# Fill the fourth tile of query rows up to whole groups, load queries one tile ahead, and issue the second scatters behind the first splits

## The chip, the cores and the metric

One core of one Trainium2 chip runs the program. The metric is the device time of one execution in microseconds. Engines work beside each other and wait for one another through semaphores: TensorE (PE, with its weight loads as PEld), VectorE (DVE), ScalarE (ACT), GpSimd (POOL) and SyncE (SP). DMA transfers are issued from the queues of SP and ACT; an issue takes the queue some time, and an issue that waits holds up all that stand behind it in that queue.

## What is computed

Attention whose heads are mixed by a 12 x 12 matrix before the softmax and by another one after it, followed by two feed-forward layers on its output (4 x 448 tokens, 768 wide).

```
scores = scale * np.matmul(q, k.transpose(0, 1, 3, 2))     # 4 batches, 12 heads, 448 x 448, head size 64
scores = np.einsum('bhij,hg->bgij', scores, w_pre)
scores = scores - np.max(scores, axis=-1, keepdims=True)
attn = np.exp(scores)
attn = attn / (np.sum(attn, axis=-1, keepdims=True) + 1e-09)
attn = np.einsum('bhij,hg->bgij', attn, w_post)
x = np.matmul(attn, v)
...
x = (1.0 / (1.0 + np.exp(-(x @ w_gate))) * (x @ w_val)) @ w_out
h = np.maximum(x @ w_in, 0.0)
out = (h * h) @ w_out2
```

## The kernel before

The mixing over heads is a matrix product whose contraction runs over (row, head) pairs: ten query rows (GI = 10) times twelve heads fill 120 partitions, with a block-diagonal matrix as weight. Such ten rows are a *group*. A batch of 448 rows is cut into four *tiles* of 110, 110, 110 and 118 rows (`row_tiles`); the first three are eleven groups each, the fourth eleven groups and one of eight rows. Two tiles are a *chunk*, for which the value products run together.

`scores(n, p)` makes the scores of tile n for the pair of heads p: two products into PSUM, a copy of each to an SBUF buffer `e` (one on ScalarE, one on VectorE), and a *scatter* of each, a DMA from `e` (a row of the tile on each partition) into `g` (a partition for each row-in-group and head, the groups one behind the other). So that a scatter is one regular access, the host lays the query rows out in the order of `row_order`: first the row 0 of all groups, then row 1, and so on. Where the tile has rows beyond whole groups, they follow at the end, and a second small DMA (line 196, the *tail*) scatters them. The very first tile is laid out as two blocks (groups 0 to 3 and 4 to 10), whose second scatters are collected in the list `second` and issued later (line 357), so that the first groups can start early.

`split(s)` then takes group s of `g` apart into a high and a low half (`gh` on ScalarE, `gl` on GpSimd), `premix(s)` makes three products of them, `maximum`, `exponent` and `normal` the softmax, `postmix(s)` the mixing after it, and `values(c, h)` the value products of chunk c for a pair of heads, with `vraw` from `v_load`: two heads a buffer, four buffers, so of the six loads of a chunk the fifth and sixth wait for the first and second pair of value products. `valued` copies the result out (`xo`) and stores it to DRAM (`xs`).

The order of everything is written out by hand, in a loop over s, the groups of all batches. Each step issues the premix of group s, the split of group s + 2, and, as its budget of TensorE time allows, postmixes, value products and the scores of the next tile; `next_scores` issues the scores of a pair of heads and, in the fourth tile of a batch, behind them a load of `k` for the next batch. In that loop the queries of tile n + 1 are loaded (`q_load`, two buffers) behind the last pair of heads of tile n. Nearly all DMAs go through SyncE's queue in the order of the program; only some scatters of the very first tile are issued by ScalarE. The feed-forward part (`mlp`) is fed into the last steps of that loop and then runs alone.

Of the kernel before, what the change touches and what calls it, by code (L numbers as in the profile page):

```python
# [18 lines left out]
GI = 10  # L19
# [17 lines left out]

def blocks(b, i0, i1):

    n = (i1 - i0) // GI  # L40
    return [(0, 4), (4, n)] if b == i0 == 0 else [(0, n)]


def row_order(b, i0, i1):

    rows = []
    for g0, g1 in blocks(b, i0, i1):
        rows += [i0 + g * GI + r for r in range(GI) for g in range(g0, g1)]
    return rows + list(range(i0 + len(rows), i1))


def attention(tc, q, k, v, w_pre, w_post, xs, B, H, S, D):
# [10 lines left out]
    nc = tc.nc  # L63
    JT = S // JP
    NP = H // 2
    SCALE = 1.0 / float(D) ** 0.5

    tiles, groups, chunks = [], [], []
# [7 lines left out]
            chunks[-1][4] = len(groups)  # L76
            tiles.append((b, i0, i1 - i0))
    NG = len(groups)
    IM = max(t[2] for t in tiles)
    GT = -(-IM // GI)  # L80
    CM = max(c[2] - c[1] for c in chunks)
    KM = GI * H

    with ExitStack() as ctx, ExitStack() as mid, ExitStack() as left:
# [55 lines left out]
        k_t, q_t = {}, {}  # L140
# [3 lines left out]
            nc.sync.dma_start(out=k_t[b, p], in_=k[b, p])  # L144

        def q_load(n, p0=0, p1=NP):
            b, i0, isz = tiles[n]
            if p0 == 0:
                q_t[n] = p2.tile([P, NP, IM], F32, tag="q", name="q")
            n0, n1 = (b * S + i0) * H * D, (b * S + i0 + isz) * H * D  # L150
            x = q[n0:n1].rearrange("(d p i) -> d p i", d=P, p=NP)
            nc.sync.dma_start(out=q_t[n][:, p0:p1, :isz], in_=x[:, p0:p1])


        g_t, second = {}, []

        def scores(n, p):

            b, i0, isz = tiles[n]
            if p == 0:  # L160
                g_t[n] = pg.tile([KM, GT, S], F32, tag="g", name="g")
            kt = k_t.pop((b, p)) if i0 + isz == S else k_t[b, p]
            ps = [
                ps_b.tile([P, S], F32, tag="b", name="ps_s")
                if n == 0 and p % 2
                else ps_q.tile([P, S], F32, tag="q", name="ps_s")
                for _ in range(2)
            ]
            for o in range(2):
                r = slice(o * D, (o + 1) * D)  # L170
                nc.tensor.matmul(  # L171
                    ps[o][:isz], lhsT=q_t[n][r, p, :isz], rhs=kt[r], start=True, stop=True
                )
            if n == 0 and p >= 3:
                e = [pa.tile([IM, S], F32, tag="a", name="e0") for _ in range(2)]
            else:
                t = p4.tile([IM, 2, S], F32, tag="e", name="e")
                e = [t[:, o] for o in range(2)]
            to = g_t[n].rearrange("(r h) g j -> h r g j", h=H)
            for o in range(2):  # L180
                if o:
                    nc.vector.tensor_copy(e[o][:isz], ps[o][:isz])
                else:
                    nc.scalar.copy(e[o][:isz], ps[o][:isz])
                e0 = 0
                for m, (g0, g1) in enumerate(blocks(b, i0, i0 + isz)):
                    e1 = e0 + (g1 - g0) * GI
                    move = (to[2 * p + o, :, g0:g1], e[o][e0:e1])
                    if m:
                        second.append(move)  # L190
                    else:
                        queue = nc.scalar if n == 0 and o and p in (1, 3, 4, 5) else nc.sync
                        queue.dma_start(out=move[0], in_=move[1])
                    e0 = e1
                if e0 < isz:
                    nc.sync.dma_start(out=to[2 * p + o, : isz - e0, g1], in_=e[o][e0:isz])


        a_t = {}
# [109 lines left out]
        NT = len(tiles)  # L309
# [24 lines left out]
        def next_scores():  # L334
            _, _, n, h = front.pop(0)
            scores(n, h)
            if tiles[n][1] + tiles[n][2] == S:
                load_next(k_load, k_order)
            if h == NP - 1 and n + 1 < NT:
                q_load(n + 1)  # L340

        def flush():
# [4 lines left out]
        for p in range(0, NP, 2):  # L347
            q_load(0, p, p + 2)
            load_next(k_load, k_order)
            load_next(k_load, k_order)  # L350
        q_load(1)
        masks()
        for p in range(NP):
            scores(0, p)
        mixers()
        for m, (x, y) in enumerate(second):
            (nc.scalar if m % 3 == 1 else nc.sync).dma_start(out=x, in_=y)  # L357
        for s in range(2):
            split(s)
        for s in range(NG + 30):  # L360
            if s < NG:
                premix(s)
            flush()
            if s < NG:
                maximum(s)
            if s in (4, 5, 6, 7):
                load_next(v_load, v_order)
            if 8 <= s < 8 + KB - NP:
                load_next(k_load, k_order)
            if 1 <= s <= NG:  # L370
                exponent(s - 1)
            if 2 <= s < NG + 2:
                normal(s - 2)
            if s + 2 < NG:
                split(s + 2)
            left_over = STEP - MW
            ready = front and front[0][0] <= s
            if ready and due(s):
                next_scores()
                ready, left_over = False, left_over - SW  # L380
            while bpos < len(back) and (left_over > 0.5 or s >= NG):
                f, cost, *x = back[bpos]
                if f is postmix:
                    if x[0] > s - LAG:
                        break
                    posted[groups[x[0]][3]] = s
                elif posted[x[0]] == s:
                    if s < NG:
                        break
                    flush()  # L390
                elif posted[x[0]] == s - 1 and ready:
                    next_scores()
                    ready = False
                if len(pending) > 3:
                    flush()
                f(*x)
                if f is values and (x[1] + 2) % HV == 0:
                    pending.append((load_next, v_load, v_order))
                bpos += 1
                left_over -= cost  # L400
                if f is postmix and x[0] == NG - 1:
                    flush()
                    mid.close()
                if s >= NG:
                    yield 3 if bpos == len(back) or back[bpos][0] is values else 2
            if ready and left_over > 0.4:
                next_scores()
            if not front and not closed:
                left.close()
                closed = True  # L410
            if NG - EARLY <= s < NG:
                behind += 1
                if closed:
                    yield 2
                elif behind >= 3 and s not in posted.values():
                    behind -= 3
                    yield 1
# [406 lines left out]
```

## Time and profile before

| | |
|---|---|
| median of three runs | 1508.63 us (1508.27 to 1511.84) |
| profiled execution | 1510.66 us, of it 1508.9 us span |
| PE busy | 1468.7 us, 97% of the span |
| PE on the chain that ended last | 95% |
| DVE, ACT, POOL busy | 809.2, 579.6, 708.8 us |
| DMA | 185.47 MB in 87976 packets, 123 GB/s in the mean |

TensorE is busy in nearly the whole span, so the profile is read for the places where it waits. The page gives shares of the whole; the stage in question, attention, takes about the first 540 us, and there the timelines, the waits and the stretches tell more. In a timeline a row is an instruction, or several alike merged (x16), with its start and length; a bracket at its end says how long its engine was idle before it and what released it. Where a wait had several reasons, the bracket names one of them, which need not be the one that came last.

### The profile page before, as it was taken

To read this page: it belongs to the slowest core of one execution; us is meant where nothing else is said; L and a number is where in the kernel's file an instruction comes from. 1 tells how busy PE (TensorE), PEld (TensorE's weight loads), DVE (VectorE), ACT (ScalarE), POOL (GpSimd) and SP (SyncE) were. 2 spreads that over 40 slices of the span, in tenths; PEclk is the share of its full clock that TensorE was granted. 3 is DMA by queue.
4 is the path that set the end of the run, shared out by engine and by line. 5 is a ranking of instruction groups with operands and counts; after the bars stand their busy time and mean duration, and the time that the engine had idled before them with its cause. 6 is when DMAs were issued, how large, how long until landed. Compare 5 with 4: busy or idle time off the path is not lost.

```text
span 1508.9 us, 22075 instructions
## 1 busy us (share of the span) xinstructions
PE 1468.7 (97%) x8028; PEld 1245.0 (83%) x8028; DVE 809.2 (54%) x1367; ACT 579.6 (38%) x1192; POOL 708.8 (47%) x583
## 2 busy tenths in 40 slices
PE   6989989999998999999999999999999999999999
PEld 3657657667676889999999999999999999999998
DVE  4648657667678577778889999911111001333000
ACT  4545645655655333333234433312222122333111
POOL 3646656766679355555455555532222221222221
PEclk8989999999999999999999999999999999999999
DMA  5453553545534354444444446631211111112221
GB/s 178 140 163 113 150 156 119 168 132 172 167 116 141 113 170 174 156 166 164 158 157 159 163 166 205 217 96 53 63 43 62 53 53 53 53 53 67 75 72 39
DMA packets 87976, 185.47 MB, mean 123 GB/s; under 512 B 18236, under 2 KB 55100, under 8 KB 87868
## 3 DMA queue, kind: packets, MB, share of 16 engines
q1 hardware_dynamic: 87348, 183.28, 38.4%
q8 instruction: 63, 1.03, 0.3%
q10 hardware_dynamic: 520, 0.79, 0.2%
q14 instruction: 45, 0.37, 0.1%
HBM read 107.75 MB, written 37.75 MB: 96 GB/s over the span
## 4 chain that ended last, share of the span: by engine, by line
PE 95%; DMA 2%; POOL 1%; DVE 1%; issue 1%; SPq 0%; ACT 0%; ACTq 0%; POOLq 0%; DVEq 0%
PE ps L666 66%; PE ps_p L261 9%; PE ps_m L219 8%; PE ps_s L171 6%; PE ps_v L290 5%; DMA vraw<-in_v 1%; DMA q<-in_q 0%; POOL gl L210 0%; POOL wn L246 0%; DMA g<-e 0%; DVE ap L273 0%; DMA k<-in_k 0%; ACTq L357 0%; POOL wl L534 0%; DVE nm L227 0%
## 5 line engine op out<-in xcount | busy, mean ns | idle before, releaser
L534 POOL TENSOR_TENSOR wl<-w,wh 128x768 fp32r<-128x768 f32 (+1 forms) x140 | 257.6, 1842 | 550.8 <-ACT wh L526 542.4
L666 PE MATMUL ps<-xh,wh 128*128 128x448 f32 x960 | 351.1, 366 | 0.0
L666 PE MATMUL ps<-xh,wl 128*128 128x448 f32 x960 | 350.7, 365 | 0.0
L666 PE MATMUL ps<-xl,wh 128*128 128x448 f32 x960 | 350.6, 365 | 0.0
L666 PE MATMUL ps<-hh,wl 128*128 128x448 f32 x672 | 246.8, 367 | 0.0
L666 PE MATMUL ps<-hl,wh 128*128 128x448 f32 x672 | 246.8, 367 | 0.0
L666 PE MATMUL ps<-hh,wh 128*128 128x448 f32 x672 | 246.7, 367 | 0.0
L210 POOL TENSOR_TENSOR gl<-g,gh 120x448 fp32r<-120x448 f32 x180 | 208.6, 1160 | 22.2 <-DMA g<-e 18.6
L261 PEld LDWEIGHTS ps_p<-wn,a 120*112 120x112 f32 (+1 forms) x1440 | 165.0, 178 | 43.2 <-issue 20.7
L666 PEld LDWEIGHTS ps<-xh,wh 128*128 128x128 f32 x960 | 180.3, 188 | 15.5 <-issue 1.0
L666 PEld LDWEIGHTS ps<-xh,wl 128*128 128x128 f32 x960 | 180.3, 188 | 14.4 <-POOL wl L534 0.2
L666 PEld LDWEIGHTS ps<-xl,wh 128*128 128x128 f32 x960 | 180.3, 188 | 14.2
L261 PE MATMUL ps_p<-wn,a 120*112 120x120 f32 (+1 forms) x1440 | 177.0, 271 | 6.9 <-POOL wn L246 6.8
L246 POOL TENSOR_SCALAR wn<-wq,sm 120x120 f32<-120x120 f32 x180 | 107.2, 596 | 148.9 <-DVE sm L244 115.4
L520 POOL TENSOR_TENSOR w<-w,w_f 128x768 f32<-128x768 f32 (+1 forms) x70 | 135.4, 1934 | 59.0 <-DVE w_f L509 59.0
L227 DVE TENSOR_REDUCE nm<-ps_m 120x1 f32<-120x448 f32 x180 | 112.0, 622 | 78.9 <-PE ps_m L219 78.6
L684 DVE TENSOR_TENSOR ps<-ps,sg 128x448 f32<-128x448 f32 x48 | 30.4, 632 | 197.2 <-PE ps L666 197.2
L666 PEld LDWEIGHTS ps<-hl,wh 128*128 128x128 f32 x672 | 126.1, 188 | 11.6
L666 PEld LDWEIGHTS ps<-hh,wh 128*128 128x128 f32 x672 | 126.1, 188 | 11.6
L666 PEld LDWEIGHTS ps<-hh,wl 128*128 128x128 f32 x672 | 126.1, 188 | 11.6
L235 ACT ACTIVATE a<-ps_m,nm 120x448 f32<-120x448 f32 x180 | 115.0, 639 | 48.0 <-DVE nm L227 46.6
L273 DVE COPY ap<-ps_p 112x480 f32<-112x480 f32 x180 | 117.0, 653 | 27.2 <-PE ps_p L261 27.2
(45 smaller groups left out, 1693.7 us busy)
## 6 DMA issues: line engine op xcount, KB each, us to landing
g<-e SPq DMA_DIRECT2D x180, 192.5 KB
ws<-w SPq DMA_DIRECT2D x58, 384.0 KB
w<-ws SPq DMA_DIRECT2D x58, 384.0 KB
w_raw<-in_wo SPq DMA_DIRECT2D x18, 768.0 KB
w_raw<-in_wi SPq DMA_DIRECT2D x16, 768.0 KB
vraw<-in_v SPq DMA_DIRECT2D x48, 224.0 KB
w_raw<-in_wg SPq DMA_DIRECT2D x12, 768.0 KB
w_raw<-in_wv SPq DMA_DIRECT2D x12, 768.0 KB
```

The source lines that it names most:

```text
L171: nc.tensor.matmul(ps[o][:isz], lhsT=q_t[n][r, p, :isz], rhs=kt[r], start=True, stop=True)
L210: nc.gpsimd.tensor_tensor(out=lo[:kk], in0=x, in1=hi[:kk].bitcast(F32), op=ALU.subtract)
L219: nc.tensor.matmul(ps[:kk], lhsT=wp[w][:kk, :kk], rhs=x, start=m == 0, stop=m == 2)
L227: nc.vector.tensor_reduce(out=nm[:kk], in_=ps[:kk], op=ALU.max, axis=AX.X, negate=True)
L235: nc.scalar.activation(a[:kk], ps[:kk], AF.Exp, bias=nm[:kk], accum_out=sm[:kk])
L246: nc.gpsimd.tensor_scalar(out=wn[:kk], in0=wq[:kk], scalar1=sm[:kk], scalar2=None, op0=ALU.mult)
L261: nc.tensor.matmul(ps[:JP, jt], lhsT=a[:kk, jt * JP : (jt + 1) * JP], rhs=wn[:kk].rearrange("p g i -> p (g i)"), start=True, stop=True,)
L273: nc.vector.tensor_copy(ap[c][:, :, :, g0 - i0 : g0 - i0 + rows], ps[:JP, :, :, :rows])
L290: nc.tensor.matmul(ps[o * D : (o + 1) * D, :w], lhsT=vraw[c, (h + o) // HV][:, (h + o) % HV, jt, :], rhs=ap[c][:, jt, h + o, :w], start=jt ...
L520: nc.gpsimd.tensor_tensor(out=x[:, s], in0=x[:, s], in1=fs.pop(n)[:, s], op=ALU.add)
L534: nc.gpsimd.tensor_tensor(out=lo[:, s], in0=w32.pop(n)[:, s], in1=h[:, s].bitcast(F32), op=ALU.subtract)
L666: nc.tensor.matmul(ps, lhsT=a, rhs=x, start=first and n == 0, stop=last and n == total - 1)
```

## The change

The fourth tile becomes twelve whole groups. `row_order` repeats the last row of the tile where a group runs over its end, so the host lays out 120 rows for 118; the queries are loaded, multiplied, copied and scattered with these two extra rows, and one scatter a head carries all of it. The tail DMA is gone. The mixing of the twelfth group goes on using its eight real rows.

In the loop, the queries of tile n + 1 are loaded behind the first pair of heads of tile n instead of the last. The queries of the second tile of all are loaded behind the first tile's scatters instead of ahead of them.

At the start, the second scatters of the first tile are issued behind the first two splits instead of ahead of them, and ScalarE issues two of them (the fourth and the eighth) instead of four.

```diff
 def blocks(b, i0, i1):
 
-    n = (i1 - i0) // GI
+    n = -(-(i1 - i0) // GI)
     return [(0, 4), (4, n)] if b == i0 == 0 else [(0, n)]
...
     for g0, g1 in blocks(b, i0, i1):
-        rows += [i0 + g * GI + r for r in range(GI) for g in range(g0, g1)]
-    return rows + list(range(i0 + len(rows), i1))
+        rows += [min(i0 + g * GI + r, i1 - 1) for r in range(GI) for g in range(g0, g1)]
+    return rows
...
-    IM = max(t[2] for t in tiles)
-    GT = -(-IM // GI)
+    full = [-(-t[2] // GI) * GI for t in tiles]
+    IM = max(full)
+    GT = IM // GI
...
         def q_load(n, p0=0, p1=NP):
-            b, i0, isz = tiles[n]
...
-            n0, n1 = (b * S + i0) * H * D, (b * S + i0 + isz) * H * D
+            n0, isz = sum(full[:n]) * H * D, full[n]
+            n1 = n0 + isz * H * D
...
         def scores(n, p):
 
-            b, i0, isz = tiles[n]
+            b, i0, rows = tiles[n]
+            isz = full[n]
...
-                for m, (g0, g1) in enumerate(blocks(b, i0, i0 + isz)):
+                for m, (g0, g1) in enumerate(blocks(b, i0, i0 + rows)):
...
-                if e0 < isz:
-                    nc.sync.dma_start(out=to[2 * p + o, : isz - e0, g1], in_=e[o][e0:isz])
...
-            if h == NP - 1 and n + 1 < NT:
+            if h == 0 and n + 1 < NT:
                 q_load(n + 1)
...
-        q_load(1)
         masks()
         for p in range(NP):
             scores(0, p)
+        q_load(1)
         mixers()
-        for m, (x, y) in enumerate(second):
-            (nc.scalar if m % 3 == 1 else nc.sync).dma_start(out=x, in_=y)
         for s in range(2):
             split(s)
+        for m, (x, y) in enumerate(second):
+            (nc.scalar if m in (3, 7) else nc.sync).dma_start(out=x, in_=y)
```

The first place is the end of the fourth tile of the first batch in SyncE's queue, from its fifth pair of heads on. A row is an issue, destination and source with their numbers, and the destination's shape; L193 is a scatter, L196 a tail, L144 a load of `k`, L152 of `q`, L306 the store of a value result, L280 a load of `vraw`. Before:

```order
L193 DMA g_821<-e_1001 10x11x448
L196 DMA g_821<-e_1001 8x448
L193 DMA g_821<-e_1001 10x11x448
L196 DMA g_821<-e_1001 8x448
L144 DMA k_1008<-in_k 128x448
L152 DMA q_1010<-in_q 128x6x110
L306 DMA xs0_57<-xo_1025 128x220
L280 DMA vraw_1028<-in_v 112x512
L306 DMA xs0_57<-xo_1056 128x220
L280 DMA vraw_1059<-in_v 112x512
```

In the same queue now (the line numbers are those of the changed kernel):

```order
L198 DMA g_821<-e_964 10x12x448 x2
L148 DMA k_969<-in_k 128x448
L198 DMA g_821<-e_993 10x12x448 x2
L148 DMA k_998<-in_k 128x448
L309 DMA xs0_57<-xo_1013 128x220
L283 DMA vraw_1016<-in_v 112x512
L309 DMA xs0_57<-xo_1044 128x220
L283 DMA vraw_1047<-in_v 112x512
```

Ahead of the fifth `vraw` load two tails a pair of heads are gone, and the load of `q`, which has moved up to the tile's first pair.

The second place is SyncE's queue at the start, from the last first-block scatter of the first tile to the scatters of the second. Before (the second tile's `q` was issued earlier, ahead of `wr`, as the row `q_146`):

```order
L193 DMA g_153<-e0_205 10x4x448
L357 DMA g_153<-e_158 10x7x448
L357 DMA g_153<-e_167 10x7x448 x2
L357 DMA g_153<-e_176 10x7x448
L357 DMA g_153<-e0_185 10x7x448
L357 DMA g_153<-e0_195 10x7x448
L357 DMA g_153<-e0_196 10x7x448
L357 DMA g_153<-e0_206 10x7x448
L193 DMA g_247<-e_252 10x11x448 x2
L193 DMA g_247<-e_274 10x11x448 x2
```

Now:

```order
L198 DMA g_151<-e0_203 10x4x448
L156 DMA q_209<-in_q 128x6x110
L362 DMA g_151<-e_156 10x7x448 x2
L362 DMA g_151<-e_165 10x7x448
L362 DMA g_151<-e_174 10x7x448 x2
L362 DMA g_151<-e0_183 10x7x448
L362 DMA g_151<-e0_193 10x7x448
L362 DMA g_151<-e0_194 10x7x448
L362 DMA g_151<-e0_203 10x7x448
L362 DMA g_151<-e0_204 10x7x448
L198 DMA g_247<-e_252 10x11x448 x2
L156 DMA q_257<-in_q 128x6x110
```

The second tile's `q` (`q_209`) now stands behind the first block, ten second scatters in place of eight follow it, and the third tile's `q` (`q_257`) stands behind the second tile's first two scatters.

The third place is ScalarE at the start, where its second-block scatters stood ahead of the first casts `gh`. Before:

```order
L193 DMA g_153<-e0_206 10x4x448
L357 DMA g_153<-e_158 10x7x448
L357 DMA g_153<-e_176 10x7x448
L357 DMA g_153<-e0_186 10x7x448
L357 DMA g_153<-e0_205 10x7x448
L209 CAST gh_229<-g_153 120x448
L209 CAST gh_233<-g_153 120x448
```

Now:

```order
L198 DMA g_151<-e0_204 10x4x448
L212 CAST gh_217<-g_151 120x448
L212 CAST gh_221<-g_151 120x448
L362 DMA g_151<-e_165 10x7x448
L362 DMA g_151<-e0_184 10x7x448
```

Two casts come first, and two second scatters follow in place of four.

## Rows read from the trace of the kernel before

**Rows 1.** Waits of PE: engine, line, waited for: us in total, times, longest

```profile
PE ps_v L290 <- DMA vraw<-in_v: 13.9, 4, 7.0
PE ps_m L219 <- ACT gh L209: 8.0, 1, 8.0
PE ps_s L171 <- DMA q<-in_q: 2.5, 1, 2.5
```

**Rows 2.** Timeline of PE, fourth tile, first batch: start us, us, engine, line, operation

```profile
83.12 1.02 PE L171 MATMUL ps_s<-k,q 64*118 64x448 f32 x4
...
88.95 1.71 PE L290 MATMUL ps_v<-ap,vraw 112*64 112x220 f32 x16
...
91.39 1.71 PE L290 MATMUL ps_v<-ap,vraw 112*64 112x220 f32 x16
...
100.89 3.20 PE L290 MATMUL ps_v<-ap,vraw 112*64 112x220 f32 x16 [7.00 <-DMA vraw<-in_v]
...
108.59 1.80 PE L261 MATMUL ps_p<-wn,a 120*112 120x120 f32 x16
```

**Rows 3.** Timeline of SP's queue: the start, and the fourth tile's end

```profile
5.18 0.67 SPq L152 DMA_DIRECT2D q<-in_q  x1
...
16.75 6.68 SPq L357 DMA_DIRECT2D g<-e  x8
...
89.15 0.77 SPq L193 DMA_DIRECT2D g<-e  x1
89.97 0.66 SPq L196 DMA_DIRECT2D g<-e  x1
90.73 0.39 SPq L144 DMA_DIRECT2D k<-in_k  x1
...
94.85 0.62 SPq L152 DMA_DIRECT2D q<-in_q  x1
...
96.24 0.38 SPq L280 DMA_DIRECT2D vraw<-in_v  x1
```

**Rows 4.** Timeline of PE, second and third batch, the same place

```profile
214.48 1.71 PE L290 MATMUL ps_v<-ap,vraw 112*64 112x220 f32 x16
...
228.57 1.80 PE L261 MATMUL ps_p<-wn,a 120*112 120x120 f32 x16
...
334.48 1.71 PE L290 MATMUL ps_v<-ap,vraw 112*64 112x220 f32 x16
...
345.68 1.80 PE L261 MATMUL ps_p<-wn,a 120*112 120x120 f32 x16
```

**Rows 5.** Timeline of PE, first scores of the third tile

```profile
45.27 1.46 PE L171 MATMUL ps_s<-k,q 64*110 64x448 f32 x4 [2.53 <-DMA q<-in_q]
...
49.42 1.01 PE L171 MATMUL ps_s<-k,q 64*110 64x448 f32 x4
...
51.97 1.01 PE L171 MATMUL ps_s<-k,q 64*110 64x448 f32 x4
```

**Rows 6.** Timeline of ACT: the start, the twelfth group's cast, a value copy

```profile
14.09 3.40 ACTq L357 DMA_DIRECT2D g<-e  x4
19.81 1.50 ACT L209 CAST gh<-g 120x448 fp32r<-120x448 f32 x3 [6.09 <-DMA g<-e]
...
44.01 0.56 ACT L209 CAST gh<-g 120x448 fp32r<-120x448 f32 x1 [2.58 <-POOL wn L246]
...
86.22 0.35 ACT L305 COPY xo<-ps_v 128x220 f32<-128x220 f32 x1
```

**Rows 7.** The chain that ended last, 0 to 50 us: start us, us, what

```profile
38.17 7.05 DMA q<-in_q
```

**Rows 8.** Stretches: us, busy by engine (instructions), granted PE clock, DMA share, GB/s

```profile
30.00:40.00 10.00, 9.77 (x64) 6.91 (x64) 8.22 (x20) 7.20 (x18) 7.42 (x10) 1.00 0.70 207
...
84.00:94.00 10.00, 9.89 (x78) 6.10 (x76) 3.65 (x14) 5.59 (x17) 6.59 (x8) 1.00 0.60 183
...
101.00:109.00 8.00, 8.00 (x43) 5.17 (x44) 1.06 (x4) 2.42 (x8) 1.68 (x2) 0.62 0.31 87
```

More of the change, by code (lines that the diff above doesn't have):

```diff
@@ L157, in scores @@
         def scores(n, p):
-            b, i0, isz = tiles[n]
+            b, i0, rows = tiles[n]
+            isz = full[n]
             if p == 0:
                 g_t[n] = pg.tile([KM, GT, S], F32, tag="g", name="g")
-            kt = k_t.pop((b, p)) if i0 + isz == S else k_t[b, p]
+            kt = k_t.pop((b, p)) if i0 + rows == S else k_t[b, p]
             ps = [
```

## The prediction

> **What bounds the kernel now.** TensorE is busy nearly everywhere, so I looked first for the places where it is not: the waits of TensorE [rows 1]. Three of its entries touch the change: four waits of the value products on `vraw` (13.9 us in all, the longest 7.0), one of the score products on `q` (2.5 us), and the first mix, held 8.0 us by the first cast `gh`, which itself waits for the first scatters. I then took each place in the timelines.
>
> *Fourth tile of a batch.* The value products of the chunk before run at the end of the fourth tile's scores, one pair of heads every 2.44 us (88.95 to 91.39, [rows 2]). Four pairs have their `vraw` in SBUF. The fifth load can be issued once the first pair is done; it should run at 91.39 + 2.44 = 93.83 and runs at 100.89. After the wait its 16 products take 3.20 us in place of 1.71: TensorE's granted clock, 0.62 in the mean from 101 to 109 [rows 8], is at its lower level, 1.2 GHz, for most of that stretch. The first double mix-back starts at 108.59; at three steps of 2.44 it would start at 98.71. This place costs **9.88 us**. Why is `vraw` late? SyncE's queue [rows 3] issues back to back: a scatter takes 0.82 us of it (89.15 to 89.97), its tail of eight rows 0.76 (89.97 to 90.73) for a fourteenth of the bytes. A pair of heads, four issues and a `k` load of some 0.45 (0.39 and the gap), takes 3.6 us of queue against the 2.56 us in which TensorE makes a pair of scores (49.42 to 51.97, [rows 5]), so the queue falls behind by about 1 us a pair, six times; then comes the `q` load (94.85), a store, and `vraw` at 96.24. The store's source was copied out at 86.22 to 86.57 [rows 6]. So `vraw` stood in line for over 9 us, and its landing (100.89 less 96.24, 4.65 with the wake-up) comes on top.
>
> *The same place in the next batches* [rows 4]: 228.57 − 214.48 = 14.09 in place of 7.32 is a loss of **6.77**; 345.68 − 334.48 = 11.20 is **3.88**; the fourth batch has next to nothing, the small rest of the 13.9 us. The loss shrinks with the number of transfers in the queue (the third batch has two `k` loads, the fourth none), which is what a queue that is too slow would do.
>
> *Third tile of the first batch* [rows 5, 7]: its `q` is issued at 38.17, behind all scatters of the second tile, and lands 7.05 us later; the scores wait 2.53 us and the next step takes 4.15 us (45.27 to 49.42) in place of 2.56, again at a lower clock: 2.53 + 1.59 = **4.12**.
>
> **The change part by part.** My sums are made against the profiled execution's own 1510.66 us; the median of the runs shown, 1508.63, is 2.03 lower, and I take that off at the end.
>
> *Fill-up.* The tails go: 12 × 0.76 = 9.1 us of SyncE's queue in each fourth tile. What is left for a pair is two scatters at 0.82 and the `k` load, 2.1 us, under the 2.56 us of TensorE's step. The queue then waits for the score copies, and at the end of the tile it is one pair behind at most. The other half of the term is the `q` load, which no longer stands directly ahead of the stores (0.6 us). The last scores of the tile run at 83.12 [rows 2]; about 1 us for the copies, 2.1 for the queue and 0.5 for the store put `vraw` at about 87.5. With 4.65 us to land it is there at 92.2, ahead of 93.83; the sixth is asked for 2.4 us later and wanted 2.4 us later. So the stalls of the first three batches go whole: **9.88 + 6.77 + 3.88 = 20.5 us**. What is late next at that place is nothing that I can see: the fourth batch, which has almost no stall, runs on at the same step. The wider rows cost nothing: four products for 118 rows take 1.02 us [rows 2], for 110 rows 1.01 [rows 5]; the two repeated rows go through otherwise idle partitions, and the scatter grows from 110 to 120 runs of 1792 B, some 18 KB a head less 14 KB of tail.
>
> *Queries a tile ahead.* For the third tile of the first batch `q` is issued after the second tile's first scatters, at about 26.6 (the second block's issues end at 16.75 + 6.68 = 23.4 today, 2.35 later then by the next paragraph, and 0.84 for a scatter) instead of 38.17, and even with 7.05 us it is there by 34, against 42.7. But the wait that takes its place is in the trace: ScalarE's cast of the second tile's first group ran at 44.01 after 2.58 us of idle [rows 6]. The row names POOL, which had long been done; what it needs is the last scatter of the second tile. The `q` transfer now goes ahead of that scatter, and behind the cast ScalarE has the copy that frees the scores' banks. If the scatter lands as before, the following step starts as early as it can and all 4.12 is won. If it lands 1.6 us later (the `q` transfer's 338 KB at the 207 GB/s of that stretch, [rows 8]), the cast (0.56) ends at 46.2, a copy of about the same length at 46.7, and the step that stood at 49.42 starts there: 2.7 won. I take the middle, **3.4**.
>
> *Start.* Today ScalarE issues four second-block scatters (14.09, 3.40 us long) among the last first-block scatters that release the first cast at 19.81 [rows 6]. Behind the splits they are out of that way, and the second tile's `q` (0.67 us of the queue at 5.18, [rows 3]) no longer stands ahead of the first scatters: at best 3.4 us are won. Against it, SyncE now has ten second scatters and `q` behind the first block instead of eight (16.75, 6.68 us, 0.84 each): 2 × 0.84 + 0.67 = 2.35 us later for the second block, which the fifth group needs, so at worst 2.4 are lost. Both happen: the first four groups start earlier and then wait for the fifth. I take the middle, **0.5**. For the second tile's `q` itself: if it is issued at about 15 and takes 7.05 us at worst, it lands at 22, some 2 us behind today's first cast and about when the first mix is through; it costs nothing on the old schedule, though it may take the whole of the gain.
>
> *Sum*: 20.5 + 3.4 + 0.5 = 24.4. 1510.66 − 24.4 = 1486.3, and in terms of the median **1484 us**.
>
> **Rivals.**
>
> *The transfers take the place of the queue (1490).* Without the tails a pair of heads asks for 2 × 215 KB of scatter and 229 KB of `k` in 2.56 us, 257 GB/s. From 30 to 40 us, where the same mixture lands ever later (7.05 us for `q`), the trace shows 207 GB/s [rows 8]. At that rate a pair takes 3.18 us, six pairs end 3.7 us late, and `vraw` lands at 95.9 in place of 92.2: a stall of 2.1 and, as above, 2.9 for the clock, 5.0 in the first batch. In the second batch the load stands ahead of the sixth pair's scatters, so five pairs count and the margin is some 1.2 us larger: 5 × 0.62 − 2.8 leaves about 1 with the clock. The third has two `k` loads and fits. That gives back 6: 1490. At the 183 GB/s of 84 to 94 (3.6 us a pair) it is 4.6 + 2.9 and 2.4 + 2.4, 12 in all: 1496. That is the end of this rival, since there the queue and not the transfers set the rate. For it speaks 207; against it, that the 207 also held stretches that the queue left empty, and the DMA share was 0.70.
>
> The Trainium skill, "DMA: Bandwidth & Descriptors", section "Why a DMA increments its semaphore by 16 and not by 1", speaks for this rival: a transfer runs on the largest number of engines up to 16 that divides the slowest dimension of both sides, so filling 110 rows up to 120 still leaves ten engines, each with twelve runs in place of eleven. By the rate per engine of that page's "Specifications" (about 27 GiB/s) an estimate for a pair and its `k` load is some 2.0 us, which would fit; the measured 207 GB/s would not. The trace's share of 0.70 agrees with idle engines, and no row settles the rate.
>
> *The gain at the third tile turns into the scatter's wait (1488).* The second block lands 2.4 us later, the second tile's scatters follow, and the cast of 44.01 slides with them: the 3.4 and 0.5 become zero or less. 1484 + 4 = 1488.
>
> *Slower (1522).* The first rival with a worse rate. At 145 GB/s a pair takes 4.55 us; the first batch stalls for 6 × 1.99 − 1.6 + 2.9 = 13.2, the second for 5 × 1.99 − 2.8 + 2.4 = 9.6, the third for about 2: the 24.4 are used up, so from there on it decides. At 120 GB/s (5.5 us) the three are 18.9, 14.3 and 5.1, 38.3 in all: 1484 + 38 = 1522. Speaks against it: 183 GB/s with the tails in between.
>
> *The change doesn't do what it says:* a load that still waits on something else, for instance on a buffer of `vraw`. The buffer is free once the first pair's products end, before their copy at 86.22, so I see no such wait. The time would stay at 1508.
>
> **How the numbers follow.** Forecast 0.60, transfers 0.20, scatter's wait 0.13, slower 0.03, no effect 0.04. The forecast's own range, from 4.12 and 3.4 won at the two last terms to 2.7 and −2.4, is 1480 to 1488. The range reaches to the first rival's larger part: 1479 to 1494. The measurement of this kernel tells about 0.3% (4.5 us) from no change. All but the last two cases are faster by more: faster 0.93, within 0.3% 0.04, slower 0.03.
>
> **What would show it.** In the profile after: TensorE's waits on `vraw` and `q` gone or under 1 us; SyncE idle between the pairs of the fourth tile, and `vraw` issued within 2 us of the first value copy; three steps of 2.44 between the fourth pair of values and the first double mix-back; the granted clock at its upper level there. A `vraw` that is issued at 88 and lands after 94 is the first rival. A cast idle until after 44 with the scores behind it is the second. The forecast is wrong if the fourth tile's queue is not the cause, that is if `vraw` is issued early and TensorE still waits, or if the start loses more than the 2.4 us.

## The result, and the profile after

The changed kernel takes 1494.93 us in the median (1494.55 to 1495.32) against 1509.18 for the kernel before on the same chip: ratio 0.9906 [0.9889, 0.9922], 14.2 us won. Forecast were 24.4 us and 1484, with a range up to 1494. The profiled execution took 1494.55 us, 1492.8 of it span; by the prediction's way of counting that stands against 1486.3, so 8.3 us are missing in it. (Between the medians 10.9 are missing: the 2.03 us that the sum takes off, since the profiled execution before lay above its median, have no counterpart here, where the profiled execution lies 0.4 below.)

The waits of TensorE in the changed kernel, with one of VectorE (engine, line, waited for: us in total, times, longest), to be laid beside [rows 1]:

```profile
PE ps_m L222 <- ACT gh L212: 5.6, 1, 5.6
PE ps_v L293 <- DMA vraw<-in_v: 4.5, 2, 2.4
PE ps_s L176 <- ACT e L189: 2.5, 3, 1.6
...
DVE e L187 <- DMA g<-e: 11.9, 9, 2.3
```

The wait on `q` is gone, that on the first cast `gh` is 2.4 us shorter, that on `vraw` has gone from 13.9 to 4.5 us, where under 1 was forecast. A new one stands below it: scores that wait for a copy to an `e` buffer, and the copies in turn wait for scatters out of these buffers (`g<-e`) to land.

TensorE's timeline at the third tile, in the fourth tiles of the first three batches and at the mix-backs behind them (start us, length, engine, line, operation), which answers [rows 2, 4, 5]:

```profile
42.59 1.01 PE L176 MATMUL ps_s<-k,q 64*110 64x448 f32 x4
...
45.14 2.07 PE L176 MATMUL ps_s<-k,q 64*110 64x448 f32 x4
...
48.76 1.01 PE L176 MATMUL ps_s<-k,q 64*110 64x448 f32 x4
...
82.00 1.12 PE L176 MATMUL ps_s<-k,q 64*120 64x448 f32 x4 [1.55 <-ACT e L189]
83.05 1.71 PE L293 MATMUL ps_v<-ap,vraw 112*64 112x220 f32 x16
...
90.36 1.71 PE L293 MATMUL ps_v<-ap,vraw 112*64 112x220 f32 x16
...
95.29 3.19 PE L293 MATMUL ps_v<-ap,vraw 112*64 112x220 f32 x16 [2.42 <-DMA vraw<-in_v]
...
99.36 1.71 PE L293 MATMUL ps_v<-ap,vraw 112*64 112x220 f32 x16
...
101.70 1.80 PE L264 MATMUL ps_p<-wn,a 120*112 120x120 f32 x16
...
207.54 1.71 PE L293 MATMUL ps_v<-ap,vraw 112*64 112x220 f32 x16
...
212.09 1.71 PE L293 MATMUL ps_v<-ap,vraw 112*64 112x220 f32 x16 [2.04 <-DMA vraw<-in_v]
...
216.87 1.80 PE L264 MATMUL ps_p<-wn,a 120*112 120x120 f32 x16
...
322.71 1.71 PE L293 MATMUL ps_v<-ap,vraw 112*64 112x220 f32 x16
...
329.92 1.29 PE L264 MATMUL ps_p<-wn,a 120*112 120x120 f32 x11
```

Read against the rows of before at the same work, the gain grows like this: 3.21 us at the third score pair of the third tile (51.97 to 48.76); only 1.03 at the fourth pair of values of the first batch (91.39 to 90.36), since the scores at 82.00 have waited; 6.89 at the first double mix-back (108.59 to 101.70); 11.70 at the second (228.57 to 216.87); 15.76 at the third (345.68 to 329.92); 16.1 at the end of the span. The third batch is clean, 7.21 us from the fourth pair to the mix-back. The first still takes 11.34 in place of 7.32, the second 9.33: 4.02 and 2.01 us of the stalls are left.

SyncE's queue at the start and at the end of the fourth tile, which answers [rows 3]:

```profile
14.51 0.66 SPq L156 DMA_DIRECT2D q<-in_q  x1
15.22 9.17 SPq L362 DMA_DIRECT2D g<-e  x10
...
84.76 1.64 SPq L198 DMA_DIRECT2D g<-e  x2
86.50 0.46 SPq L148 DMA_DIRECT2D k<-in_k  x1
87.84 0.34 SPq L309 DMA_DIRECT2D xs<-xo  x1
88.27 0.38 SPq L283 DMA_DIRECT2D vraw<-in_v  x1
```

The queue has gaps, as the prediction said, and `vraw` is issued at 88.27 in place of 96.24, 0.8 us behind the forecast 87.5. What happens after the issue is late, and the gaps are no free time, as the chain that ended last in the changed kernel shows (start, us, what):

```profile
72.97 6.76 DMA g<-e
...
79.80 8.39 DMA k<-in_k
...
88.27 6.88 DMA vraw<-in_v
```

`vraw` takes 6.9 us to land, where the prediction put 4.65 from before. A `k` load of that tile takes 8.4 us, a scatter 6.8. The `k` load and `vraw` are each issued within 0.1 us of the landing of the one ahead of them in the chain (72.97 + 6.76 = 79.73, 79.80 + 8.39 = 88.19). In the trace's records the transfers of this queue signal their landing on eight semaphores in turn, and an issue waits until the transfer eight places ahead, which uses the same semaphore, has landed. Of the ten gaps of over 0.3 us in the queue from 79 to 95 us seven end that way, one with that or with a freed `vraw` buffer, and two with score copies that had themselves waited 2.7 and 1.2 us for a scatter out of their `e` buffer. In the kernel before no issue waits like this from 74 to 99 us. So the queue, which is no longer slow in itself, is now held by the landings. And the stretches that answer [rows 8] (us, busy by engine with instructions, granted clock of TensorE, DMA share, GB/s):

```profile
76.00:88.00 12.00, 10.45 (x68) 5.99 (x68) 5.91 (x17) 6.11 (x16) 6.51 (x8) 1.00 0.79 205
...
84.00:94.00 10.00, 8.87 (x70) 5.33 (x64) 4.02 (x13) 6.23 (x17) 6.41 (x9) 1.00 0.84 244
...
94.00:100.00 6.00, 4.71 (x27) 3.24 (x29) 0.54 (x1) 1.42 (x4) 1.57 (x2) 0.72 0.36 113
```

205 GB/s while the kernel asks for 257 is the first rival's picture, though TensorE's scores stood for 1.55 us within that stretch, and from 84 to 94 the same execution moves 244. From 94 to 100 the granted clock is 0.72, so it again falls behind the stall.

### The profile page after: what moved, and what is told of

It is laid out like the page before. It is cut to its first block, busy times and chain, and to the rows that moved or that the text cites. A ratio compares the mean times of both kernels' runs of the same rounds, so it can differ in the third digit from the quotient of the medians.

```text
span 1492.8 us, 21984 instructions
## 1 busy us (share of the span) xinstructions
PE 1464.9 (98%) x8028; PEld 1242.1 (83%) x8028; DVE 808.3 (54%) x1367; ACT 579.8 (39%) x1192; POOL 709.6 (48%) x583
## 3 DMA queue, kind: packets, MB, share of 16 engines
q8 instruction: 63, 1.03, 0.3%
## 4 chain that ended last, share of the span: by engine, by line
PE 92%; DMA 4%; POOL 2%; issue 1%; DVE 1%; ACT 0%; SPq 0%; POOLq 0%; ACTq 0%; DVEq 0%
PE ps L669 67%; PE ps_p L264 8%; PE ps_m L222 7%; PE ps_s L176 5%; PE ps_v L293 5%; DMA g<-e 2%; DMA k<-in_k 1%; POOL gl L213 1%; DMA vraw<-in_v 1%; POOL wn L249 1%; DMA q<-in_q 0%; DVE ap L276 0%; ACT e L189 0%; POOL wl L537 0%; DVE nm L230 0%
## 5 line engine op out<-in xcount | busy, mean ns | idle before, releaser
L669 PEld LDWEIGHTS ps<-xl,wh 128*128 128x128 f32 x960 | 180.3, 188 | 14.2
```

The lines of the kernel that those rows point to most:

```text
L669: nc.tensor.matmul(ps, lhsT=a, rhs=x, start=first and n == 0, stop=last and n == total - 1)
```

## The experiments

Theory **T**: in the fourth tile the kernel asks for more bytes than the transfers give; what lands late is late for that. Theory **R**: something in the order of the queue, above all the next batch's queries at the head of the fourth tile, or the edit at the start, costs the missing gain.

### The three edits one by one

The fill-up alone (the change without the two moves of `q_load` and without the move of the second scatters):

> The kernel before with the fill-up alone: whole groups in the fourth tile, one scatter a head; the queries and the second scatters at the start stay where they were. The changed kernel gained 14.25 us, at its own places: about 2.7 by the third tile, 4.2, 4.8 and 4.0 in the fourth tiles of the first three batches. Theory T (what is left of the stalls is transfers: a pair of heads asks for more than the transfers give): the fourth tiles gain as in the changed kernel, so 13 us less than before, about 1496, with the wait on q in the third tile (2.5 us) back. Theory R (what is left comes from the queries of the next batch standing at the head of the fourth tile, ahead of its scatters): with the queries at the tile's end again the scatters run earlier, but the q load stands ahead of the fifth vraw again; the e wait of the sixth score pair goes, and some 5 us more are won: about 1491.

Measured: 1494.42 us (1491.18 to 1501.74), ratio 0.9911 [0.9889, 0.9934], 13.4 us won. The median is nearer to T's 1496 than to R's 1491, but the executions spread over both answers, so it decides little.

The queries alone:

```diff
-            if h == NP - 1 and n + 1 < NT:
+            if h == 0 and n + 1 < NT:
```

> The kernel before with the queries loaded a tile ahead alone. In the changed kernel the third tile of the first batch gained about 2.5 us against the start. Theory T: the same here, 1506; the stalls on vraw stay as before or shorten by the 0.6 us that q no longer takes of SyncE's queue there: 1505 to 1506. Theory R (queries at the fourth tile's head do harm): the vraw stalls grow by as much as is won: 1509.

Measured: 1508.14 us, ratio 0.9987 [0.9978, 0.9997]: 2.0 us won, T's value to within 2. (The kernel before itself spreads from 1505.2 to 1512.8 us on that chip, so single executions tell nothing here.) The wait on `q` is gone from its waits of TensorE, and the one on `vraw` is what it was:

```profile
PE ps_v L290 <- DMA vraw<-in_v: 14.0, 4, 5.5
```

The start alone:

```diff
-        q_load(1)
         for p in range(NP):
             scores(0, p)
+        q_load(1)
...
-        for m, (x, y) in enumerate(second):
-            (nc.scalar if m % 3 == 1 else nc.sync).dma_start(out=x, in_=y)
         for s in range(2):
             split(s)
+        for m, (x, y) in enumerate(second):
+            (nc.scalar if m in (3, 7) else nc.sync).dma_start(out=x, in_=y)
```

> The kernel before with the start's edit alone: second scatters behind the first two splits, the second tile's q behind the first tile's scores. My prediction gave it 0.5 us of gain (between a loss of 2.4 and a gain of 3.4). In the changed kernel the first mix-back starts 0.95 us earlier and the second tile's second score pair only 0.2 earlier, so I expect 0 to 1 us of gain: 1508 to 1509. If instead the start is what costs the missing gain, this run is slower by 1 us or more.

Measured: 1508.10 us, ratio 0.9989 [0.9979, 1.0]: 1.7 us won, at most 3.2 and at least nothing. The start doesn't cost the missing gain. The three gains add to 17.1 us, above the 14.2 of all three edits together; by their intervals that is no contradiction.

The changed kernel again, on the chip on which the `k` loads were moved (below):

> The changed kernel again, unaltered, beside the next three: the runs of the fill-up alone spread over 10 us on their chip (1491 to 1502), those of the changed kernel over less than 1 us. If the time that a stall on vraw costs depends on whether TensorE's granted clock falls behind it, executions of one kernel fall into groups some 3 to 8 us apart, and the changed kernel shows them too: a median of 1495 with single runs some us below or above. If the spread belongs to the fill-up alone, these stay within 1 us of 1495.

Measured: 1493.66 us (1492.57 to 1497.51), ratio 0.9904 [0.9886, 0.9922]. Its profiled execution moved 239 GB/s in the stretch where the first one moved 205, and its stall in the first batch is shorter, the one in the second longer:

```profile
92.61 1.71 PE L293 MATMUL ps_v<-ap,vraw 112*64 112x220 f32 x16 [1.24 <-DMA vraw<-in_v]
...
208.59 3.20 PE L293 MATMUL ps_v<-ap,vraw 112*64 112x220 f32 x16 [2.81 <-DMA vraw<-in_v]
```

So one kernel's executions differ in how late the transfers are and in whether the clock falls behind a stall: 16 products took 1.71 us after 1.24 and 2.04 us of idle time, 3.19 and 3.20 after 2.42 and 2.81. That is the spread of some us seen above.

### Taking bytes out of the fourth tile

The changed kernel with the next batch's queries behind the value products:

```diff
-            if h == 0 and n + 1 < NT:
+            if h == 0 and n + 1 < NT and tiles[n][1] + tiles[n][2] < S:
                 q_load(n + 1)
...
+                if f is values and x[1] == H - 2 and x[0] % 2 == 0 and 2 * x[0] + 4 < NT:
+                    pending.append((q_load, 2 * x[0] + 4))
```

> The changed kernel, with the queries of the next batch's first tile loaded behind the sixth pair of value products instead of at the head of the fourth tile. Theory T (transfers are what the fourth tile lacks): 338 KB less ahead of vraw, 1.6 to 1.8 us at the rate of that stretch, in the first two batches, so the stalls on vraw shrink by about that each: 1491. Theory R (only order in SyncE's queue counts, and vraw was already issued in time): nothing changes, 1495.

Measured: 1487.36 us (four executions from 1486.9 to 1488.2, the profiled one 1495.58), ratio 0.9861 [0.9841, 0.9881]: some 6.5 us better than the changed kernel, more than T's 4. The number set down for R above, 1495, is missed; but R as it is put at the head of this section blames these very queries, and the edit moves them and their bytes at once, so it speaks against neither theory. The trace is that of the execution at 1495.58 and still has a stall on `vraw`, so it doesn't show what the other four won:

```profile
93.14 3.20 PE L293 MATMUL ps_v<-ap,vraw 112*64 112x220 f32 x16 [2.71 <-DMA vraw<-in_v]
```

The changed kernel with the `k` loads behind the value products:

```diff
-            if tiles[n][1] + tiles[n][2] == S:
-                load_next(k_load, k_order)
...
                     pending.append((load_next, v_load, v_order))
+                    if x[0] % 2 == 0:
+                        pending.append((load_next, k_load, k_order))
```

> The changed kernel, with the k loads of the next batch issued behind the value products of the chunk before, one for each pair, and no longer behind each score pair of the fourth tile. Theory T (transfers are what the fourth tile lacks): of the 660 KB that a score pair asks for, 229 go; the scatters land as in the third batch, which has two k loads and no stall, vraw lands 4 us earlier or more, and both the waits on vraw and the score pair's wait for a free e buffer go: 1.7 + 4 in the first batch and 2 in the second, about 1487. Theory R (order in SyncE's queue): vraw is already issued at 88, nothing is won: 1495.

Measured: 1485.89 us (1485.02 to 1487.90), ratio 0.9849 [0.9833, 0.9865], beside the changed kernel on the same chip 7.8 us less. T holds, R falls: the queries stand where they stood. TensorE's timeline of this kernel at the end of the fourth tile is what the prediction described, an even step of 2.44 us and no bracket:

```profile
88.56 1.71 PE L293 MATMUL ps_v<-ap,vraw 112*64 112x220 f32 x16
...
91.00 1.71 PE L293 MATMUL ps_v<-ap,vraw 112*64 112x220 f32 x16
...
93.44 1.71 PE L293 MATMUL ps_v<-ap,vraw 112*64 112x220 f32 x16
...
95.78 1.80 PE L264 MATMUL ps_p<-wn,a 120*112 120x120 f32 x16
```

Its stretches show what the same engines move once no scatter is among the transfers (88 to 92 us, `k`, `vraw` and stores): 285 GB/s at full share, against 205 at a share of 0.79.

```profile
88.00:92.00 4.00, 4.00 (x34) 2.54 (x35) 1.70 (x6) 2.73 (x8) 2.61 (x3) 1.00 1.01 285
```

Both moves together:

> The changed kernel with both moved: the k loads behind the value products, and the next batch's first queries behind the sixth pair of value products. Theory T: once the k loads are away the transfers fit, so the queries' move adds little: 1486 to 1487, no wait of TensorE on vraw in any batch, granted clock at its upper level from 90 to 110 us. Had each transfer its own price on the path, the two gains would add: the 7.6 us of the queries' move alone (1487.4) and as much again. Theory R: 1495 or what the queries' move alone gave.

Measured: 1489.80 us (1487.79 to 1493.78), ratio 0.9876 [0.9856, 0.9896]. A miss: the waits on `vraw` are gone, but the queries now come too late, and the scores of the next batch wait for them:

```profile
PE ps_s L176 <- DMA q<-in_q: 5.6, 2, 3.5
```

Bytes, or places in the queue? The `k` loads moved away, and at their old place loads of 8 columns of 448 that nothing uses:

```diff
+            if tiles[n][1] + tiles[n][2] == S and tiles[n][0] + 1 < B:
+                x = pz.tile([P, 8], F32, tag="z", name="z")
+                nc.sync.dma_start(out=x, in_=k[tiles[n][0] + 1, h][:, :8])
...
```

> The changed kernel with the k loads of the next batch behind the value products, and at their old place behind each score pair of the fourth tile a load of 8 of the 448 columns (4 KB in place of 229), never used; it stands at all six pairs of the first three batches. If the bytes bind, this runs as without it, 1486, and vraw causes no wait. If places bind (a turn in SyncE's queue, one of the transfers that may be under way at a time), the stalls come back: 1493 to 1495.

Measured: 1486.25 us, ratio 0.9849 [0.9835, 0.9864]. The places cost nothing, the bytes do. That answers a third theory too, that the eight semaphores bind and not the bytes: as many transfers stand in the fourth tile as in the changed kernel, and between 68 and 102 us no issue of SyncE waits for a landing. Whether more than eight transfers at a time would raise the rate no run tests.

### Taking the wait away and leaving the bytes

The changed kernel with all six `vraw` loads of the chunk issued ahead (`v_times` moves the triggers of these loads forward):

```diff
+        pvx = left.enter_context(tc.tile_pool(name="a_vx", bufs=2, side="left"))
...
-            t = pv4.tile([JP, HV, JT, D], F32, tag="vraw", name="vraw")
+            p = pvx if c in (0, 2, 4) and hv >= 4 else pv4
+            t = p.tile([JP, HV, JT, D], F32, tag="vraw", name="vraw")
...
-            if s in (4, 5, 6, 7):
+            if s in (4, 5, 6, 7, 12, 13):
...
-                    pending.append((load_next, v_load, v_order))
+                    for _ in range(v_times(x[0], x[1] // 2)):
+                        pending.append((load_next, v_load, v_order))
```

> The changed kernel with all six vraw loads of the chunk in front of the first three fourth tiles issued ahead (two more buffers), so that no value product waits on a load issued in that stretch; scatters, k and q stay. Theory T: the waits on vraw (4.0 and 2.1 us with the clock behind them) go, the score pair's wait for an e buffer (1.7) stays: about 1489. If instead the transfers hold the scores too, as the e waits say, part of it comes back as longer e waits: 1490 to 1493.

Measured: 1489.06 us (1488.64 to 1491.52), ratio 0.9871 [0.9855, 0.9887], T's number. No wait on `vraw` is left. The score pairs' waits add to a little more than in the changed kernel, but the one in the first batch's fourth tile is 0.70 us in place of 1.55; the others stand elsewhere:

```profile
PE ps_s L177 <- ACT e L190: 3.3, 6, 1.1
```

The same loads ahead in the kernel before, tails and all:

> The kernel before, its tails still there, with all six vraw loads of the chunk in front of the first three fourth tiles issued ahead (two more buffers). If the whole loss at the fourth tiles is that vraw is late, as my prediction had it, the 20.5 us go without the fill-up: 1509 - 20.5 = 1488.5. If the crowded queue also holds the scores (a score pair waits for an e buffer whose scatter has not landed), part of it comes back there: 1491 to 1495.

Measured: 1499.26 us, ratio 0.9934 [0.9921, 0.9947]. Both numbers miss. TensorE waits on `vraw` for 0.2 us in all, yet some 10 us of the 20.5 are still lost. In the first batch the trace shows what else is late behind the crowded queue: the stores. ScalarE's copy of a value result waits for a store to free its `xo` buffer, the softmax of the groups queues up behind that copy, and TensorE stands for it and then works at a granted clock of 0.66 in the mean from 96 to 106 us:

```profile
98.53 0.34 ACT L307 COPY xo<-ps_v 128x220 f32<-128x220 f32 x1 [5.69 <-DMA xs<-xo]
...
99.56 1.10 PE L220 MATMUL ps_m<-gh,wp 120*120 120x448 f32 x2 [3.31 <-ACT a L236]
```

How much of the 10 us is the stores' in the later batches was not taken apart.

### Queue or transfers, before and after

The kernel before with only the `k` loads moved behind the value products:

> The kernel before, its tails still there, with the k loads of the next batch behind the value products. By my prediction's reading (SyncE's queue binds before: four issues, 3.16 us, and 0.45 for k, against 2.56 us of scores) the queue still falls behind, by 0.6 us a pair in place of 1.0: of the 9.88 us in the first batch 2.7 go, of the 6.77 in the second 2.2: 1504. If the transfers bound the kernel before as well, these and the 229 KB a pair go: all or most of the 20.5, 1489 to 1493.

Measured: 1499.50 us, ratio 0.9936 [0.9923, 0.9948], between the two numbers. Its SyncE queue is never free in the fourth tile, one head after the other in 1.58 us, 3.16 a pair against 2.56:

```profile
88.49 0.77 SPq L193 DMA_DIRECT2D g<-e  x1
89.31 0.67 SPq L196 DMA_DIRECT2D g<-e  x1
90.07 0.61 SPq L152 DMA_DIRECT2D q<-in_q  x1
90.78 0.59 SPq L306 DMA_DIRECT2D xs<-xo  x1
91.47 0.37 SPq L280 DMA_DIRECT2D vraw<-in_v  x1
```

while the DMA engines are half idle:

```profile
76.00:88.00 12.00, 12.00 (x82) 7.40 (x82) 7.59 (x21) 7.80 (x21) 7.62 (x9) 1.00 0.48 136
```

So with the tails the queue binds, as the prediction read it; `vraw` is issued 4.8 us earlier than in the kernel before and TensorE still waits 3.2 us for it:

```profile
95.40 3.20 PE L290 MATMUL ps_v<-ap,vraw 112*64 112x220 f32 x16 [3.21 <-DMA vraw<-in_v]
```

Without them the transfers bind, and the two limits lie close together.

The changed kernel with the odd head's scatter of the fourth tiles on ScalarE's queue:

```diff
-                        queue = nc.scalar if n == 0 and o and p in (1, 3, 4, 5) else nc.sync
+                        act = o and (p in (1, 3, 4, 5) if n == 0 else i0 + rows == S)
+                        queue = nc.scalar if act else nc.sync
```

> The changed kernel, with the odd head's scatter of each fourth tile issued on ScalarE's DMA queue in place of SyncE's; the same transfers and bytes. If the DMA engines behind the queues bind (ten of them for a scatter), a second queue gives nothing in the fourth tile: 1494, and it may lose a little since ScalarE issues between its casts. If one queue is what gives only some 207 GB/s, the transfers land earlier and the stalls shrink: 1488 to 1491.

Measured: 1488.91 us (1487.54 to 1490.76), ratio 0.9866 [0.9851, 0.9881]: some 5 us better than the changed kernel with no byte saved. The rate in the stretch is 265 GB/s, just above the 257 that are asked for:

```profile
76.00:88.00 12.00, 11.96 (x85) 7.28 (x85) 6.33 (x18) 7.80 (x22) 8.15 (x10) 1.00 0.83 265
```

Is it the second queue as such? The `k` loads on ScalarE's queue in place of the scatters (`nc.scalar.dma_start` for them, nothing else):

> The changed kernel, with the k loads of the fourth tiles issued on ScalarE's DMA queue in place of SyncE's; both scatters stay in SyncE's queue, and no byte is saved or moved in time. If one queue that carries all is what gave only 205 to 239 GB/s there, a second one helps whatever it carries: some 265 GB/s from 76 to 88 us as with the odd scatters moved, the vraw wait nearly gone, 1488 to 1490. If the gain with the odd scatters moved came from something in the scatters (issued side by side, earlier by one turn of the queue), this stays at 1493 to 1495. It may also be slower: a k load on ScalarE waits behind that engine's copies.

Measured: 1497.23 us (1494.66 to 1503.51), ratio 0.9917 [0.9898, 0.9937]. No. The trace is that of the slowest of the six executions, 1503.51: with a second queue for the `k` loads its rate is 188 GB/s, and in the fourth tile the scores wait 2.6 us for the scatters to free their buffers, against 1.55 in the changed kernel (which in turn asks for less while they wait, so part of the low rate is of the stall's making).

```profile
PE ps_s L180 <- ACT e L193: 4.2, 2, 2.6
```

```profile
76.00:88.00 12.00, 9.37 (x50) 5.03 (x49) 5.53 (x15) 4.43 (x12) 5.38 (x7) 0.86 0.63 188
```

SyncE's own waits say why (engine, line, waited for: us in total, times, longest):

```profile
SPq L202 <- DMA k<-in_k: 12.6, 2, 6.3
```

In the first and in the second batch its queue stands for 6.3 us, each time until a `k` load of the other queue has landed, which signals on the semaphore that the next scatter is to use. So a second queue doesn't help whatever it carries. Why scatters that are issued side by side go better stays open. The Trainium skill, "DMA: Bandwidth & Descriptors", section "Queues, rings and completion order", says that a DMA engine takes turns between the queues that have work for it; by that a `k` load on its own queue would push in between the scatters, which agrees with the longer wait for them, but no run here shows the turns.

Both remedies, `k` late and odd scatters on ScalarE's queue:

> The changed kernel with the k loads behind the value products, and with the odd head's scatters of the fourth tile on ScalarE's queue. With the k loads away TensorE waits for no transfer in the fourth tiles, so a second queue has nothing left to give: 1486, within a microsecond of the k move alone (1485.9). If the remaining 0.7 us of waits for an e buffer and the start vary with the queue, up to 1 us more is won; if ScalarE's issues stand ahead of its casts, up to 2 us are lost.

Measured: 1486.63 us, ratio 0.9847 [0.9831, 0.9863], as with the `k` loads late alone. With these away no value product waits on `vraw`, so there is next to nothing to add. The kernel with the `k` loads late beats both kernels; the second queue on top of it isn't needed.

## Why the prediction was off

**What bounds the kernel before: right.** SyncE's queue, not the transfers, made `vraw` late: with the `k` loads away it still ran without a gap while the engines' share was 0.48. That other things are late behind the same queue (the stores) the prediction didn't see; the kernel before with early `vraw` shows it.

**Fill-up, 20.5 us: the step that failed.** It was the sentence that with 4.65 us to land `vraw` "is there at 92.2, ahead of 93.83; ... So the stalls of the first three batches go whole". The issue came as forecast (88.27). But the landing time was taken from the kernel before, where the slow queue kept the engines at a share of 0.60; with the queue freed the transfers pile up, and it was 6.88 us. Eight transfers of some 220 KB at 205 to 244 GB/s are, as an estimate, 7.2 to 8.6 us, and with eight under way at a time that is what a landing takes. The sentence ahead of it, "The queue then waits for the score copies", failed with it: the queue waits for landings. Measured on the traces, the first stall shrank by 5.86 us of 9.88 (17.20 to 11.34), the second by 4.76 of 6.77, the third by 3.99 of 3.88. A further loss of 2.2 between the third score pair and the value products, of which the `e` wait shows 1.55, was forecast by nothing: buffers that come free only when a scatter lands tie the scores to the same transfers. With the `k` bytes out of the way the median is 23.4 us below before, close to the 24.4; but that takes an edit that the forecast did not have, and that alone is worth 9.5 us in the kernel before.

**The first rival: right in its mechanism, and given 0.20.** It put `vraw`'s landing at 95.9 (95.15 measured), a stall of 2.1 (2.42), and 1490 to 1496 for its two rates; the measured 205 GB/s from 76 to 88 is near the 207 it started from, and the time lies in its upper half because of the `e` wait that it lacked. That its landing fits to 0.8 us is in part luck: its sum has no term for the 338 KB of the next batch's queries, which the change itself puts at the head of this tile, and loading these later won some 6.5 us. The argument that outweighed it, that the 207 held stretches which the queue left empty, is half borne out: the changed kernel also shows 244 (84 to 94 us) and 239 (in the other execution). But even these are under the 257 that it asks for. The Trainium skill, "DMA: Bandwidth & Descriptors", section "Why a DMA increments its semaphore by 16 and not by 1", pointed that way with ten of sixteen engines for a scatter; a share of 0.79 at 205 GB/s beside 1.01 at 285 without scatters agrees with it, though no row names the engines. The prediction's estimate of 2.0 us a pair, from the rate per engine that the Trainium skill gives on the same page, did not hold: 659 KB at 205 GB/s are 3.2 us, at 244 they are 2.7.

**Queries ahead, 3.4, and the start, 0.5:** 3.9 together, 3.21 measured at the third score pair of the third tile, 2.0 and 1.7 us for each alone. The first cast runs earlier and the cast of the second tile's first group runs later, as the second rival said:

```profile
17.11 0.57 ACT L212 CAST gh<-g 120x448 fp32r<-120x448 f32 x1 [3.72 <-DMA g<-e]
...
45.16 0.56 ACT L212 CAST gh<-g 120x448 fp32r<-120x448 f32 x1 [3.82 <-DMA k<-in_k]
```

It was 19.81 and 44.01 before [rows 6]; the score pair at 45.14 takes 2.07 us in place of 1.01. That rival cost about a microsecond, not four. The sum of the two terms was nearly right, with luck in it. The 4.12 us were read from one execution, in which the clock fell behind the wait on `q` (0.72 granted from 44 to 50 us). The kernels before with early `vraw` and with late `k` loads are the same as the kernel before up to there, and in their traces the clock stays up (1.00): their third score pair starts at 50.23 and 50.28, with the queries alone it starts at 50.18. Against these the changed kernel is ahead by 1.5 us. The split was not settled by these runs.

**Slower and no effect** were far off; nothing of either was seen.

## What to carry to other kernels

When a slow issue queue is freed, the landing times of the trace no longer hold: work out the bytes that the freed queue will ask for in its stretch, hold them against the best rate that the same mixture has shown, and if they exceed it take that as the forecast. Count also how many transfers may be under way at once: when all places are taken (eight here), the issue queue itself waits for landings. A load that only the next batch needs can stand behind the urgent ones; here moving the `k` loads was worth 7.8 us, and 4 KB loads in their old places cost nothing. Look at everything that comes free by a landing (store buffers, copy buffers), not only at the operand that the trace names, since taking one wait away hands the stall to the next.

## What the runs showed of the hardware that was not expected

The rate of one mixture of transfers is no constant: 205 and 239 GB/s in two executions of the same kernel from 76 to 88 us (244 in the first from 84 to 94), 265 with half of the scatters on a second queue, 188 with the `k` loads there, 285 without scatters. Part of the low ones is that stalled engines ask for less. A transfer's time to land grew to 6.8 to 8.4 us under that load, with eight transfers under way at most.
